# Splitting two layer norms between VectorE and GpSimd, with two tiny reads and another order of value rows, in a dual-stream attention block

## The chip, the cores and the metric

The kernel runs on one core of a Trainium2 chip. A core has a matrix engine (TensorE, in the profile PE, with its weight loads as PEld), VectorE (DVE), ScalarE (ACT), GpSimd (POOL) and SyncE (SP), and sixteen DMA engines that move data between HBM and the core's SBUF. The metric is the device time of one execution in microseconds (us); lower is better.

## The reference

Two streams, an image (2 x 256 tokens) and a text (2 x 32 tokens), 1152 features, all in bfloat16. Both are normalised and modulated, projected to q, k, v, attended together, projected out, gated and added to the input:

```
mod = silu(c) @ wmod                     # shift, scale, gate (image and text have their own)
h   = layernorm(x) * (1 + scale) + shift
q, k, v = split(h @ wqkv)                # image and text tokens joined
a   = softmax(q k^T / sqrt(1152)) v
out = x + gate * (a @ wo)
```

## The kernel before, in words

The instructions of each engine run in the order in which the program writes them; the tile framework adds the semaphores. The 512 image tokens are four tiles of 128 tokens (i = 0 to 3, two to a batch element, `TPB` = 2), the 1152 features nine blocks of 128 (`KT` = 9, kt = 0 to 8). All weights stream once from HBM, nearly all through SP's queue, in the order of the `dma_start` calls. An early transfer's semaphore is one of eight that are used in turn, so that a transfer waits until the one eight places ahead has landed.

The part that the change touches is the first 31 us, in which the image's values `v_i` are computed:

- Loads (lines 80 to 116): `c`, then x tiles 0 and 1 on ScalarE's queue; on SP's queue the image scale weights `w_sc_i` in four column chunks (`KC`: feature blocks 0-1, 2-3, 4-5, 6-8) and between them x tile 2, the value weights `w_v_i` by feature block and x tile 3. Blocks 6, and 7 with 8, are loaded at the end (line 110).
- Layer norm of one tile: `stats_of` (three `bn_stats`, line 169), `std_of` (aggregate on VectorE, Sqrt on ScalarE, line 176), `out_of` (line 182: reciprocal and one VectorE `tensor_scalar` from `x_i` to `xn_i`; columns can be given).
- Transposes on TensorE bring feature blocks to partitions. `x_heads(i)` transposes blocks 0 and 1 (`H` = 2) and `head_scaled` evacuates them on ScalarE with the scale applied; `x_tails(i)` transposes blocks 2 to 8 and `tail_out` copies them out of PSUM unscaled, in two pieces, for tile 0 on ScalarE and for tile 1 on VectorE. Their scale is applied later in SBUF by `apply_mod` (line 262 VectorE, 267 GpSimd, 271 ScalarE), once `mod_scale(ch)` has computed it (54 small matmuls of line 223; for the last chunk `mod_scale_last`, line 245).
- Value matmuls: `v_row(i, kt)` adds feature block kt of tile i into two PSUM banks (512 columns each, line 282); `v_narrow` does the last 128 columns of all tiles in a bank of their own (line 294). `v_wide(i, half, k0, k1)` does one bank over several blocks. PSUM tiles come from a pool of seven banks (`ps_mm`) and one further bank (`ps_sm`).
- `last_transposes` brings tile 3, whose scale is applied as VectorE evacuates it (line 309).

The order before: statistics of tiles 0 and 1, their norms, heads and tails of tile 0, heads and tails of tile 1, tail copies while tile 2 is normalised, then value rows 0 and 1 for tiles 0 and 1, heads of tile 2, second scale chunk, values of tile 2, its tails, and so on through the chunks. At the end row 6 for three tiles, then for each tile rows 7 and 8 together; the transposes of tile 3 stand behind tile 1.

Behind this stage TensorE goes on with the shift strip, the image's q and k (line 529), text rows, scores (619), attention (759) and the output (851). The weights of those stages are loaded by `load_w`, in one to three pieces (`K2` is two pieces, blocks 0-4 and 5-8; `K3` three). A tile that a piece belongs to is used when the pieces it needs have landed. `xf_full` is a tile for the text residual, 2 x 288 columns with 64 unused columns behind them.

Of the kernel before, what the change touches and what calls it, by code (L numbers as in the profile page):

```python
# [9 lines left out]
ALU = mybir.AluOpType  # L10
# [4 lines left out]
def kernel(  # L15
# [14 lines left out]
    nc = tc.nc  # L30
# [4 lines left out]
    B, NI, D = x_img.shape  # L35
    NT = x_txt.shape[1]
    P = 128
    KT = D // P
    NTOK = NI + NT
    NIT = (B * NI) // P  # L40
    TPB = NI // P
    NTT = B * NT
    CH = 384
    NCH = D // CH
# [25 lines left out]
    def w_view(src):  # L70
        return src.rearrange("(kt p) n -> p kt n", p=P)

    def load_w(src, c0, ksplits=((0, KT),), home=None):
        t = wpool.tile([P, KT, D], bf, tag="w", name="t") if home is None else act.tile([P, KT, D], bf, tag=home, name="w_home")
        for (k0, k1) in ksplits:
            nc.sync.dma_start(t[:, k0:k1, :], w_view(src)[:, k0:k1, c0:c0 + D])
        return t
# [11 lines left out]
    def load_x(i, eng=nc.sync):  # L89
        eng.dma_start(x_i[:, i, :], xi_t[:, i, :])  # L90

    def load_sc(ch):
        k0, k1 = KC[ch]
        nc.sync.dma_start(w_sc_i[:, :, k0 * P:k1 * P], w_view(wmod_img)[:, :, D + k0 * P:D + k1 * P])
# [4 lines left out]

    for i in range(TPB):  # L100
        load_x(i, nc.scalar)
    load_sc(0)
    load_x(2)
    load_v(0)
    for ch in range(1, len(KC)):
        load_sc(ch)
        if ch < len(KC) - 1:
            load_v(ch)
    for k0, k1 in ((6, 7), (7, KT)):
        nc.sync.dma_start(w_v_i[:, k0:k1, :], w_view(wqkv_img)[:, k0:k1, 2 * D:3 * D])  # L110
        if k1 < KT:
            load_x(3)
    K3 = ((0, 3), (3, 6), (6, KT))
    K2 = ((0, 5), (5, KT))
# [83 lines left out]
    def x_heads(i):  # L198
        pool, tag = (ps_sm, "sm") if i == 1 else (ps_mm, "mm")
        tp = pool.tile([P, H, P], bf, tag=tag, name="tph")  # L200
        for kt in range(H):
            nc.tensor.transpose(tp[:, kt, :], xn_i[:, i, kt * P:(kt + 1) * P], ident[:])
        return tp

    def head_scaled(tp, i):
        for kt in range(H):
            nc.scalar.activation(hT_i[:, kt, i * P:(i + 1) * P], tp[:, kt, :], ACT.Identity,
                                 scale=mod_i[:, kt, i // TPB:i // TPB + 1])

    def x_tails(i):  # L210
        pool, tag = (ps_mm, "mm") if i < TPB else (ps_sm, "sm")
        tp = pool.tile([P, KT - H, P], bf, tag=tag, name="tp")
        for kt in range(H, KT):
            nc.tensor.transpose(tp[:, kt - H, :], xn_i[:, i, kt * P:(kt + 1) * P], ident[:])
        return tp

    def tail_out(i, tp, k0, k1, on_vector=False):
        (nc.vector.tensor_copy if on_vector else nc.scalar.copy)(hT_i[:, k0:k1, i * P:(i + 1) * P], tp[:, k0 - H:k1 - H, :])
# [71 lines left out]
    def v_narrow(i, k0, k1):  # L290
        if i == 0 and k0 == 0:
            vacc["n"] = ps_mm.tile([P, NIT, P], f32, tag="mm", name="van")
        for kt in range(k0, k1):
            nc.tensor.matmul(vacc["n"][:, i, :], lhsT=hT_i[:, kt, i * P:(i + 1) * P], rhs=w_v_i[:, kt, NM:D],  # L294
                             start=(i == 0 and kt == 0), stop=(i == NIT - 1 and kt == KT - 1))

    def v_row(i, kt):
        v_wide(i, 0, kt, kt + 1)
        v_wide(i, 1, kt, kt + 1)
# [17 lines left out]
    def stats_of(i, k0, k1):  # L317
        lns[i] = ln_stats(x_i[:, i, :], P, k0, k1, lns.get(i))

    def std_of(i):  # L320
        lns[i] = ln_std(lns[i], P)

    def out_of(i, c0=0, c1=D):
        ln_apply(x_i[:, i, :], P, xn_i[:, i, :], *lns[i], c0, c1)

    stats_of(0, 0, NCH)
    std_of(0)
    stats_of(1, 0, NCH)
    std_of(1)
    out_of(0)  # L330
    mod_scale(0, "act")
    out_of(1)
    tails = []
    for i in range(TPB):
        heads = x_heads(i)
        tails.append(x_tails(i))
        head_scaled(heads, i)
    stats_of(2, 0, NCH)
    tail_out(0, tails[0], H, H + 3)
    std_of(2)  # L340
    tail_out(0, tails[0], H + 3, KT)
    tail_out(1, tails[1], H, H + 3, on_vector=True)
    out_of(2, 0, H * P)
    tail_out(1, tails[1], H + 3, KT, on_vector=True)
    out_of(2, H * P, D)
    for kt in range(*KC[0]):
        for i in range(TPB):
            v_row(i, kt)
    for i in range(TPB):
        v_narrow(i, *KC[0])  # L350
    head2 = x_heads(2)
    mod_scale(1, "dve")
    head_scaled(head2, 2)
    apply_mod(2, 0, 2, False, 0)
# [32 lines left out]
    stats_of(3, 0, NCH)  # L387
    std_of(3)
    out_of(3)
    k0 = KC[3][0]  # L390
    for i in range(3):
        v_row(i, k0)
        v_narrow(i, k0, k0 + 1)
    for i in range(3):
        for half in range(2):
            v_wide(i, half, k0 + 1, KT)
        v_narrow(i, k0 + 1, KT)
        if i == 1:
            last_transposes(0, KT - 1, ps_sm, "sm")
            last_transposes(KT - 1, KT, ps_mm, "mm")  # L400
    v_wide(3, 0, 0, KT)
    v_narrow(3, 0, KT)
# [54 lines left out]

    w_k_i = load_w(wqkv_img, D, K3)
    w_sh_t = load_w(wmod_txt, 0)
    w_sc_t = load_w(wmod_txt, D, K2)  # L460
    nc.sync.dma_start(x_t[0:P:P // NTT, :], xt_flat[:, :])
    w_q_t = load_w(wqkv_txt, 0, K2)
    w_k_t = load_w(wqkv_txt, D, K2)
    w_ga_i = load_w(wmod_img, 2 * D, K2, home="V")
    w_v_t = load_w(wqkv_txt, 2 * D, K3)
    w_o_i = load_w(wo_img, 0, K2)
    w_ga_t = load_w(wmod_txt, 2 * D)
# [461 lines left out]
```

## Time and profile before

| | |
|---|---|
| median of 3 runs | 114.62 us (114.5 to 114.75) |
| the profiled execution's own time | 114.88 us |
| its span, first to last instruction | 113.1 us |
| TensorE busy | 108.3 us (96%) |
| VectorE busy | 76.1 us (67%) |
| ScalarE busy | 36.6 us (32%) |
| GpSimd busy | 28.4 us (25%) |
| DMA | 40.87 MB, mean 361 GB/s |

The timeline gives for each group of instructions its start and length in us, the engine, the source line, the operation, output and inputs, the count, and in square brackets how long the engine stood idle before it and what ended that. "q" behind an engine's name is its sequencer, which issues transfers. A matmul's recorded length contains its latency, so neighbouring matmuls overlap in the record. The chain of waits runs backwards from the last instruction; each line of it is start, length, what.

### The profile page before, as it was taken

How to read it: one execution, taken by the hardware profiler on the slowest of the kernel's cores; microseconds unless marked ns; L12 is line 12 of the kernel's file. 1: busy time of each engine (PE TensorE's matmuls, PEld its weight loads, DVE VectorE, ACT ScalarE, POOL GpSimd, SP SyncE). 2: the span in 40 equal slices, each digit the busy share in tenths (PEclk: the TensorE clock that was granted, in tenths of full speed). 3: DMA queues.
4: the chain of work that ended last, by engine and by line, in shares of the span. 5: the costliest groups of instructions: out<-in, count | busy, mean ns of one | idle time of the engine just before them, and what ended most of it. 6: DMA issues, size and time to landing. Idle time of an engine off the chain costs nothing.

```text
span 113.1 us, 2863 instructions
## 1 busy us (share of the span) xinstructions
PE 108.3 (96%) x1195; PEld 64.0 (57%) x1204; DVE 76.1 (67%) x151; ACT 36.6 (32%) x83; POOL 28.4 (25%) x65
## 2 busy tenths in 40 slices
PE   5999999999999999999999999999999999999990
PEld 1356655555444444444446558787687556567670
DVE  1699330956399999999999950237666802995971
ACT  4537500372190071740008924025646700001000
POOL 7100120730140000000000060601550470699300
PEclk9999999999999999999999999999999999999998
DMA  3999999999999999999999999999999999994052
GB/s 92 343 333 355 375 375 405 412 411 408 407 412 412 410 411 402 413 410 412 412 411 415 408 405 407 408 392 394 407 411 397 412 408 406 371 375 161 0 191 70
DMA packets 22839, 40.87 MB, mean 361 GB/s; under 512 B 1375, under 2 KB 6635, under 8 KB 22827
## 3 DMA queue, kind: packets, MB, share of 16 engines
q1 hardware_dynamic: 21547, 39.05, 90.4%
q10 hardware_dynamic: 672, 0.77, 2.2%
q0 software_dynamic: 608, 0.88, 2.1%
q8 instruction: 9, 0.15, 0.5%
q14 instruction: 3, 0.02, 0.1%
HBM read 39.36 MB, written 1.34 MB: 360 GB/s over the span
## 4 chain that ended last, share of the span: by engine, by line
PE 80%; DMA 13%; SPq 4%; issue 1%; DVE 0%
PE qkps L529 31%; PE ps L851 16%; DMA w_sc_i<-in_wmod_img_dram 13%; PE va L282 7%; PE aps L759 5%; PE ps L590 4%; PE sps L619 4%; PE gps L429 3%; SPq L98 3%; PE ops L869 2%; PE ps L694 2%; PE van L294 1%; PE gps L824 1%; PE sps L632 1%; PE pk L703 1%
## 5 line engine op out<-in xcount | busy, mean ns | idle before, releaser
L529 PE MATMUL qkps<-hT_i,t 128*128 128x512 bf16 x158 | 35.4, 379 | 0.2
L529 PEld LDWEIGHTS <-t 128*128 128x128 bf16 x162 | 15.6, 98 | 18.7 <-issue 0.4
L491 DVE SCALAR_TENSOR_TENSOR sacc<-w_v_i,mcols,sacc 128x1152 f32<-128x1152 bf16 x16 | 22.7, 1418 | 0.5
L282 PE MATMUL va<-w_v_i,hT_i 128*128 128x512 bf16 x67 | 17.0, 379 | 0.5 <-issue 0.3
L851 PE MATMUL ps<-t,aT 128*128 128x384 bf16 x99 | 16.4, 326 | 0.0
L851 PEld LDWEIGHTS <-aT 128*128 128x128 bf16 x117 | 11.0, 98 | 6.8 <-issue 0.5
L282 PEld LDWEIGHTS <-hT_i 128*128 128x128 bf16 x72 | 6.4, 98 | 6.2 <-issue 0.2
L835 POOL TENSOR_TENSOR w_og<-t,gb 128x384 bf16<-128x384 bf16 x9 | 8.7, 999 | 4.5 <-DMA gb<-mod_scratch 4.5
L857 DVE TENSOR_TENSOR tmp<-ps,gb 128x384 bf16<-128x384 f32 x11 | 6.0, 550 | 5.6 <-DMA gb<-mod_scratch 5.0
L548 POOL TENSOR_SCALAR mod_txt<-mcols 128x18 f32<-128x18 f32 x2 | 0.6, 275 | 32.4 <-DVE mcols L435 32.4
L169 DVE BATCH_NORM_STATS2 stats<-x_i 128x6 f32<-128x384 bf16 x12 | 5.8, 541 | 2.6 <-DMA x_i<-in_x_img_dram 2.6
L143 PE MATMUL wps<-wz 128*128 128x512 bf16 x15 | 6.1, 578 | 1.2 <-DVE wz L125 1.2
L479 ACT ACTIVATE qT<-qkps 128x512 bf16<-128x512 f32 x9 | 4.7, 600 | 6.9 <-PE qkps L529 6.9
L495 ACT CAST shi<-sacc 128x1152 bf16<-128x1152 f32 x2 | 2.3, 1154 | 13.2 <-DVE sacc L491 13.2
L772 DVE TENSOR_SCALAR aT<-aps,sv 128x288 bf16<-128x288 f32 (+2 forms) x11 | 4.3, 455 | 2.0 <-PE aps L759 2.0
L590 PEld LDWEIGHTS <-t 128*128 128x128 bf16 x162 | 5.0, 98 | 0.5
L157 DVE CAST kT<-qkps 128x512 bf16<-128x512 f32 x3 | 2.1, 686 | 4.7 <-PE qkps L529 4.7
L590 PE MATMUL ps<-hT_t,t 128*128 128x64 bf16 x162 | 5.0, 193 | 0.0
L858 DVE TENSOR_TENSOR o<-tmp,x_i 128x384 bf16<-128x384 bf16 x11 | 4.7, 426 | 0.4
L759 PE MATMUL aps<-pT,v_i 128*128 128x288 bf16 (+2 forms) x44 | 4.8, 264 | 0.0
L774 ACT ACTIVATE aT<-aps,sv 128x288 bf16<-128x288 f32 (+2 forms) x11 | 4.0, 468 | 2.1 <-PE aps L759 2.1
L619 PE MATMUL sps<-kT,qT 128*128 128x288 bf16 x36 | 4.6, 286 | 0.0
(160 smaller groups left out, 139.7 us busy)
## 6 DMA issues: line engine op xcount, KB each, us to landing
t<-in_wqkv_img_dram SPq DMA_DIRECT2D x6, 864.0 KB, 13.2
t<-in_wmod_txt_dram SPq DMA_DIRECT2D x2, 2592.0 KB, 17.6
t<-in_wqkv_txt_dram SPq DMA_DIRECT2D x2, 1440.0 KB, 14.2
t<-in_wmod_img_dram SPq DMA_DIRECT2D x3, 864.0 KB, 12.3
t<-in_wqkv_txt_dram SPq DMA_DIRECT2D x3, 864.0 KB, 14.1
t<-in_wo_txt_dram SPq DMA_DIRECT2D x3, 864.0 KB, 15.5
t<-in_wqkv_txt_dram SPq DMA_DIRECT2D x2, 1152.0 KB, 15.0
w_v_i<-in_wqkv_img_dram SPq DMA_DIRECT2D x7, 288.0 KB, 6.9
```

Source lines behind the costliest of these rows:

```text
L143: nc.tensor.matmul(ps[:], lhsT=wz[:, 0:P], rhs=wz[:], start=True, stop=True)
L169: nc.vector.bn_stats(stats[0:np_, k, :], x_ap[:, k * CH:(k + 1) * CH])
L282: nc.tensor.matmul(ps[:], lhsT=hT_i[:, kt, i * P:(i + 1) * P], rhs=w_v_i[:, kt, half * VW:(half + 1) * VW], start=(kt == 0), stop=(kt == K ...
L479: nc.scalar.mul(out_ap, in_ap, SCALE)
L491: nc.vector.scalar_tensor_tensor(saccs[b][:], w_v_i[:, kt, :], ap, saccs[b][:], op0=ALU.mult, op1=ALU.add)
L529: nc.tensor.matmul(pss[j - j0][:], lhsT=wq[:, kt, j * P:(j + 1) * P], rhs=hT_i[:, kt, :], start=(kt == 0), stop=(kt == KT - 1))
L590: nc.tensor.matmul(ps[:, j - j0, :], lhsT=wq[:, kt, j * P:(j + 1) * P], rhs=hT_t[:, kt, :], start=(kt == 0), stop=(kt == KT - 1))
L619: nc.tensor.matmul(sps[:], lhsT=qkTs[0][:, ft, b, q0:q0 + P], rhs=qkTs[1][:, ft, b, :], start=(ft == 0), stop=(ft == KT - 1))
L759: nc.tensor.matmul(bank[:, off:off + c1 - c0], lhsT=lhsT, rhs=rhs, start=(first[id(bank)] == n), stop=(final[id(bank)] == n))
L835: nc.gpsimd.tensor_mul(w_og[:, dt, 0:CH], w_o_i[:, dt, NG0:D], gb[:, B - 1, NG0:D])
L851: nc.tensor.matmul(ps[:, 0:cw], lhsT=aT[:, dt, t0:t0 + P], rhs=rhs, start=(dt == DTS[0]), stop=(dt == DTS[-1]))
L857: nc.vector.tensor_mul(tmp[:, 0:cw], ps[:, 0:cw], gb[:, b, cs])
```

## The change

- Two more transfers on ScalarE's queue behind x tiles 0 and 1. Each reads 2 elements from 16 rows into unused columns of `xf_full`: every sixteenth row of x tiles 2 and 3, and every eighth of the first 128 rows of the value weights. Nothing reads what they bring.
- Value weights' feature blocks 7 and 8 are loaded one by one.
- Tiles 1 and 2: VectorE normalises columns 0 to 255 and GpSimd columns 254 to 1151. Both write columns 254 and 255, so GpSimd's instruction follows VectorE's.
- The heads of tiles 0 and 1 come first and are scaled in turn (block 0 of both, then block 1 of both). Tile 0's tails stand behind the first value row, tile 1's behind the fourth; tile 0's tail copies on ScalarE stand behind the Sqrt for tile 2.
- At the end of the value rows, row 7 of tiles 0 and 1 is done on its own ahead of row 8. The eight first transposes of tile 3 stand behind tile 0 instead of tile 1.
- Three text and gate weights (`w_sc_t`, `w_q_t`, `w_ga_i`) are loaded in one piece instead of two.

```diff
@@ -99,6 +99,8 @@
     for i in range(TPB):
         load_x(i, nc.scalar)
+    nc.scalar.dma_start(xf_full[0:16, 2 * VC + 2:2 * VC + 4], xi_flat[2 * P:4 * P:16, 0:2])
+    nc.scalar.dma_start(xf_full[0:16, 2 * VC:2 * VC + 2], wqkv_img[0:P:8, 2 * D:2 * D + 2])
     load_sc(0)
@@ -106,9 +108,9 @@
-    for k0, k1 in ((6, 7), (7, KT)):
-        nc.sync.dma_start(w_v_i[:, k0:k1, :], w_view(wqkv_img)[:, k0:k1, 2 * D:3 * D])
-        if k1 < KT:
+    for kt in range(*KC[-1]):
+        nc.sync.dma_start(w_v_i[:, kt:kt + 1, :], w_view(wqkv_img)[:, kt:kt + 1, 2 * D:3 * D])
+        if kt == KC[-1][0]:
             load_x(3)
@@ -202,8 +204,8 @@
-    def head_scaled(tp, i):
-        for kt in range(H):
+    def head_scaled(tp, i, k0=0, k1=H):
+        for kt in range(k0, k1):
@@ -323,32 +325,39 @@
+    def head_and_rest(i):
+        mv, rstd = lns[i]
+        out_of(i, 0, H * P)
+        nc.gpsimd.tensor_scalar(xn_i[:, i, H * P - 2:D], x_i[:, i, H * P - 2:D], mv[:, 0:1], rstd[:],
+                                op0=ALU.subtract, op1=ALU.mult)
+
     mod_scale(0, "act")
-    out_of(1)
-    tails = []
+    head_and_rest(1)
+    heads = [x_heads(i) for i in range(TPB)]
+    for kt in range(H):
+        for i in range(TPB):
+            head_scaled(heads[i], i, kt, kt + 1)
+    stats_of(2, 0, NCH)
+    v_row(0, 0)
+    tails = [x_tails(0)]
+    std_of(2)
+    tail_out(0, tails[0], H, H + 3)
+    tail_out(0, tails[0], H + 3, KT)
+    head_and_rest(2)
+    v_row(1, 0)
     for i in range(TPB):
-        heads = x_heads(i)
-        tails.append(x_tails(i))
-        head_scaled(heads, i)
-    stats_of(2, 0, NCH)
-    tail_out(0, tails[0], H, H + 3)
-    std_of(2)
-    tail_out(0, tails[0], H + 3, KT)
+        v_row(i, 1)
+    tails.append(x_tails(1))
     tail_out(1, tails[1], H, H + 3, on_vector=True)
-    out_of(2, 0, H * P)
     tail_out(1, tails[1], H + 3, KT, on_vector=True)
-    out_of(2, H * P, D)
-    for kt in range(*KC[0]):
-        for i in range(TPB):
-            v_row(i, kt)
+    head2 = x_heads(2)
     for i in range(TPB):
         v_narrow(i, *KC[0])
-    head2 = x_heads(2)
     mod_scale(1, "dve")
@@ -387,16 +396,20 @@
-    k0 = KC[3][0]
     for i in range(3):
-        v_row(i, k0)
-        v_narrow(i, k0, k0 + 1)
+        v_row(i, KT - 3)
+        v_narrow(i, KT - 3, KT - 2)
+    for i in range(TPB):
+        v_row(i, KT - 2)
+        v_narrow(i, KT - 2, KT - 1)
     for i in range(3):
+        k0 = KT - 1 if i < TPB else KT - 2
         for half in range(2):
-            v_wide(i, half, k0 + 1, KT)
-        v_narrow(i, k0 + 1, KT)
+            v_wide(i, half, k0, KT)
+        v_narrow(i, k0, KT)
+        if i == 0:
+            last_transposes(0, KT - 1, ps_sm, "sm")
         if i == 1:
-            last_transposes(0, KT - 1, ps_sm, "sm")
             last_transposes(KT - 1, KT, ps_mm, "mm")
@@ -457,11 +470,11 @@
-    w_sc_t = load_w(wmod_txt, D, K2)
+    w_sc_t = load_w(wmod_txt, D)
-    w_q_t = load_w(wqkv_txt, 0, K2)
+    w_q_t = load_w(wqkv_txt, 0)
-    w_ga_i = load_w(wmod_img, 2 * D, K2, home="V")
+    w_ga_i = load_w(wmod_img, 2 * D, home="V")
```

## The prediction

> **What bounds the kernel now.** I read the page first, then the chain of waits, then the timeline of the first 32 us.
>
> ```profile
> span 113.1 us, 2863 instructions
> ```
>
> ```profile
> 10.29 8.84 DMA w_sc_i<-in_wmod_img_dram
> ...
> 19.18 0.57 PE sps L245 x36
> ...
> 67.69 2.36 PE ps L590 x81
> ...
> 79.02 0.01 PE gps L636 x2
> ```
>
> The profiled run took 114.88 us, 1.78 us of them outside the span; the median of the runs is 114.62. I work out a difference on the profiled execution and add it to the median. In the chain of waits there is one large thing that is not TensorE: the last column chunk of w_sc_i, issued at 10.29 and landed 8.84 later at 19.13. TensorE's matmuls of line 245 start on it, and from there TensorE follows itself almost to the end. So an edit pays only if it lets line 245 start earlier, or shortens TensorE's own row of work behind it.
>
> ```profile
> 18.89 0.23 PE L240 MATMUL sps<-ones_full 128*32 128x96 bf16 x4
> ```
>
> This is the work in front of line 245 (timeline of TensorE). TensorE is there at 18.89 and starts at 19.18: **0.29 us of slack**. That is all that can be saved there without an earlier landing, and the first 0.29 us by which the early work becomes later cost nothing.
>
> **The early stage.** Rows of the timeline, in the order of time:
>
> ```profile
> 7.90 0.58 DVE L182 TENSOR_SCALAR xn_i<-x_i,mv,rstd 128x1152 bf16<-128x1152 bf16 x1
> ...
> 8.24 1.25 ACT L207 ACTIVATE hT_i<-tph,mod_img 128x128 bf16<-128x128 bf16 x4 [0.22 <-PE tph L202]
> 8.39 1.47 DVE L169 BATCH_NORM_STATS2 stats<-x_i 128x6 f32<-128x384 bf16 x3
> 8.53 0.11 PEld L202 LDWEIGHTS <-xn_i 128*128 128x128 bf16 x2 [0.18 <-DVE xn_i L182]
> ...
> 9.05 1.89 PE L282 MATMUL va<-w_v_i,hT_i 128*128 128x512 bf16 x7
> ...
> 9.37 0.48 ACT L218 COPY hT_i<-tp 128x384 bf16<-128x384 bf16 x1
> ...
> 10.05 0.29 DVE L218 COPY hT_i<-tp 128x384 bf16<-128x384 bf16 x1
> ...
> 10.17 0.29 ACT L176 ACTIVATE rstd<-mv,eps_t 128x1 f32<-128x1 f32 x1 [0.32 <-DVE mv L174]
> ...
> 10.37 0.57 ACT L218 COPY hT_i<-tp 128x512 bf16<-128x512 bf16 x1
> ...
> 10.70 0.34 DVE L182 TENSOR_SCALAR xn_i<-x_i,mv,rstd 128x256 bf16<-128x256 bf16 x1
> ...
> 10.96 0.42 DVE L218 COPY hT_i<-tp 128x512 bf16<-128x512 bf16 x1
> ...
> 11.23 0.59 PE L223 MATMUL mps<-sT,w_sc_i 128*128 128x2 bf16 x18
> 11.30 0.50 DVE L182 TENSOR_SCALAR xn_i<-x_i,mv,rstd 128x896 bf16<-128x896 bf16 x1
> 11.43 0.63 ACT L207 ACTIVATE hT_i<-tph,mod_img 128x128 bf16<-128x128 bf16 x2 [0.49 <-PE tph L202]
> 11.85 0.65 PE L282 MATMUL va<-w_v_i,hT_i 128*128 128x512 bf16 x2
> ...
> 12.45 0.55 PE L214 MATMUL tp<-ident,xn_i 128*128 128x128 bf16 x7
> ```
>
> A record's length holds its latency, so I use pitches. Line 282 at 9.05: eight matmuls in the code, seven recorded, the last 0.38 long: (1.89 - 0.38)/7 = 0.216 a matmul. Transposes: (0.55 - 0.22)/6 = 0.055, which I also take for the narrow matmuls (as wide). Line 223: (0.59 - 0.16)/17 = 0.025.
>
> Both orders meet again at tile 2's tail transposes, now at 12.45. From the first value matmul to there TensorE now does 8 + 2 wide matmuls (2.16), 6 narrow ones and 2 transposes (0.44), and 18 of line 223 (0.45): 3.05 us. 9.05 + 3.05 = 12.10, so 0.35 us of it is waiting.
>
> After the change the fourteen tail transposes of tiles 0 and 1 (14 x 0.055 = 0.77) stand among the value rows and not ahead of them: 3.82 us. The first value row waits for ScalarE's first scaled head: 8.24 + 1.25/4 = 8.55, and 0.10 of signal, as at 11.85, where line 282 follows the first of the two activations of 11.43 (11.43 + 0.63/2 = 11.75). Start 8.65, meeting point 8.65 + 3.82 = 12.47. **The reordering by itself is worth nothing (+0.02):** the value rows start 0.40 earlier and carry 0.77 more work; the 0.35 of waits is what it eats.
>
> Then the new waits. VectorE's part of tile 1 ends at 7.90 + 0.34 = 8.24 and not 8.48, so everything on VectorE behind it is 0.24 early: the Sqrt for tile 2 at 9.93. But ScalarE now has that Sqrt ahead of tile 0's tail copies, one of which stands at 9.37 today: 9.93 + 0.29 + 0.48 + 0.57 = 11.27 instead of 10.94. Tile 1's tails are transposed last (about 11.16), so VectorE's copies of them end near 11.45 + 0.29 + 0.42 = 12.16, and not at 10.96 + 0.42 = 11.38. The tiles `van` and `va20` need PSUM banks, and both sets of tails hold one. TensorE wants the banks at 11.27 and 12.03. If the banks freed first are taken first, it waits 0.1 and then up to 0.15 more; if `head2`'s or another is free, nothing. I take 0.2 of the 0 to 0.25: the meeting point is 12.67, 0.22 late.
>
> **GpSimd's 898 columns.** No row shows them. These do (groups by form, GpSimd):
>
> ```profile
> L835 POOL TENSOR_TENSOR w_og<-t,gb 128x384 bf16<-128x384 bf16 x9 | 8.7, 999 | 4.5 <-DMA gb<-mod_scratch 4.5
> ...
> L267 POOL TENSOR_SCALAR hT_i<-hT_i,mod_img 128x128 bf16<-128x128 bf16 x2 | 0.7, 379 | 3.3 <-DVE mod_img L231 3.3
> ...
> L267 POOL TENSOR_SCALAR hT_i<-hT_i,mod_img 128x256 bf16<-128x256 bf16 x1 | 0.5, 484 | 8.5 <-ACT hT_i L207 8.5
> ```
>
> The same operation costs (484 - 379)/128 = 0.82 ns a column: 484 + 642 x 0.82 = 1.01 us. The upper bound is the two-input rate, 999/384 = 2.6 ns: 2.3 us. The lower bound is VectorE's 0.50 for 896 columns. I take 1.01, the same operation. Tile 1: 8.35 to 9.4, wanted near 10.8: hidden. Tile 2: VectorE's head ends 0.24 earlier than 10.70 + 0.34, at 10.80; GpSimd 10.9 to 11.9, wanted at 12.47 to 12.67: hidden with 0.6 to spare. Behind it on GpSimd stands the scaling of row 3, free again before row 3's scales exist.
>
> TensorE thus reaches line 240 0.22 later, at 19.11, inside the 0.29.
>
> **The transfers.** ScalarE issues two more (0.87 us for two, below) ahead of its table loads; the first thing that can notice is the Sqrt at 5.58, which waits 0.83 for VectorE:
>
> ```profile
> 0.74 0.87 ACTq L90 DMA_DIRECT2D x_i<-in_x_img_dram  x2
> ...
> 5.58 0.29 ACT L176 ACTIVATE rstd<-mv,eps_t 128x1 f32<-128x1 f32 x1 [0.83 <-DVE mv L174]
> ```
>
> So the issuing costs 0 to 0.04. What the sixteen 4-byte reads each may bring is an earlier touch of x tiles 2 and 3 and of w_v's first row tile. Windows (the last figures are the DMA's busy share and GB/s):
>
> ```profile
> 6.30:7.60 1.30, 1.30 (x21) 0.70 (x19) 1.23 (x5) 0.29 (x1) 0.00 (x0) 1.00 1.07 353
> ...
> 18.00:19.00 1.00, 1.00 (x13) 0.62 (x12) 0.00 (x0) 0.00 (x0) 0.00 (x0) 1.00 1.05 409
> ```
>
> At the same busy share the first big packets move 353 and later ones 409 GB/s. Tile 2 and the first two value rows are 0.885 MB: 2.51 against 2.16 us. Cured wholly, 0.35 us earlier for all that follows; nothing, if the slowness is not a first touch; a loss of 0.1 (a packet in the way) below. Only a part of those bytes is touched ahead: I take 0.1. Line 245 then starts at the later of 19.08 and 19.12: **-0.06**.
>
> **The last value rows.** The same wait for normalised tile 3 gates both orders (timeline; the last two rows are the load of rows 7 and 8 and its line's times to landing):
>
> ```profile
> 21.87 0.22 PE L294 MATMUL van<-w_v_i,hT_i 128*128 128x128 bf16 x1
> 22.05 1.02 PE L282 MATMUL va<-w_v_i,hT_i 128*128 128x512 bf16 x4
> ...
> 23.00 0.58 DVE L182 TENSOR_SCALAR xn_i<-x_i,mv,rstd 128x1152 bf16<-128x1152 bf16 x1
> ```
>
> ```profile
> 13.58 0.43 SPq L110 DMA_DIRECT2D w_v_i<-in_wqkv_img_dram  x1
> ```
>
> ```profile
> DMA to landing us min/median/max: 8.4/8.7/9.0
> ```
>
> Rows 7 and 8 landed at 13.58 + 8.4 = 22.0, and line 282 started at 22.05 where 21.87 + 0.055 = 21.93 was possible: a wait of 0.12. Split, row 7 lands 295 KB earlier, 0.7 us: the wait goes. But the eight transposes of tile 3 move from behind two tiles to behind one. TensorE gets to them at 21.93 + 3 x (2 x 0.216 + 0.055) = 23.39; the tile is ready at 23.58, and 0.05 later for TensorE (8.48 to 8.53 above): a new wait of 0.24. Both chains hang on line 245 alike. **Net +0.12.** It falls to 0 if tile 3 is ready earlier.
>
> **The merged loads** cost nothing if their last half, which lands as before, is in time (page and SP's timeline):
>
> ```profile
> t<-in_wqkv_txt_dram SPq DMA_DIRECT2D x2, 1152.0 KB, 15.0
> ...
> w_home<-in_wmod_img_dram SPq DMA_DIRECT2D x1, 1152.0 KB, 14.0
> ```
>
> ```profile
> 45.51 3.21 SPq L76 DMA_DIRECT2D t<-in_wqkv_txt_dram  x2
> ```
>
> ```profile
> 59.58 2.48 SPq L76 DMA_DIRECT2D w_home<-in_wmod_img_dram  x2
> ```
>
> w_q_t: at the latest 45.51 + 3.21 + 15.0 = 63.7 against its use at 67.69. w_ga_i: 59.58 + 2.48 + 14.0 = 76.1 against 79.02. w_sc_t is ahead of w_q_t in the queue. Two transfers more, one more and three fewer leave the count, and so the turn of the later transfers' semaphores, as it was.
>
> **Sum:** -0.06 + 0.12 = +0.06. 114.62 + 0.06 = **114.7 us**: no change. A measurement of this kernel tells 0.2%, 0.23 us, from none. Bounds of this case: 114.4 to 115.0.
>
> **Rivals.** (1) *GpSimd becomes the bound* (slower). At the two-input rate the second rest ends at 10.9 + 2.3 = 13.2, the tail transposes of tile 2 start 13.3 and not 12.67, and line 240 is reached at 18.89 + 0.85 = 19.74, 0.56 past 19.18. With the 0.12: +0.68, 115.3. It decides from 12.67 on, a rest of 1.7 us or 1.9 ns a column. For it: 898 columns are far from 256. Against it: the slope of line 267. The same happens if VectorE and GpSimd hold each other up, and for that there are rows:
>
> ```profile
> L262 DVE TENSOR_SCALAR hT_i<-hT_i,scols 128x128 bf16<-128x128 bf16 x1 | 0.5, 481 | 0.0
> ...
> L262 DVE TENSOR_SCALAR hT_i<-hT_i,mod_img 128x128 bf16<-128x128 bf16 x2 | 0.4, 250 | 1.6 <-ACT hT_i L218 1.6
> ```
>
> The same VectorE instruction took 481 beside GpSimd's line 267 and 250 without. The Trainium skill (SBUF — State Buffer, "Who interferes with whom") says that the pair of ports is an exclusive lock, so that the later one blocks fully; by that rule VectorE's scaling of row 2 would stand behind the whole rest. It costs only if the rest runs past 12.3, as here. Chance, with smaller waits of that place (banks at their worst): 0.32.
>
> (2) *The touch works* (faster). Landing 0.35 earlier, no bank waits (meeting point 12.47, line 240 at 18.91, or 0.1 less if signals are shorter than mine), tile 3 ready as TensorE comes: line 245 at 18.85, -0.33, 114.3. For it: 353 against 409 GB/s. Against: it needs three terms at their good ends. 0.23.
>
> (3) *It does not do what it says*: the overlap of columns 254 and 255 orders GpSimd behind VectorE only, and the tiny reads touch nothing useful. Then the landing stays 19.13: +0.12, inside the forecast's 0.45.
>
> **Numbers.** The forecast's 0.45 splits 0.07 faster, 0.31 same, 0.07 slower; with the rivals 0.30, 0.31, 0.39. Its own range 114.4 to 115.0; the range for 8 in 10 reaches to both rivals, 114.15 to 115.4.
>
> **What would show it.** Right: first line 282 near 8.65; tile 2's tails near 12.5 to 12.7; GpSimd's rests near 1.0 us; line 245 within 0.1 of 19.1; a short idle of TensorE before line 306 at about 23.4, none before row 7. Wrong: rests over 1.7 us; the chunk landing before 18.9 or after 19.3; TensorE waiting for a merged load; the transposes of tile 3 without a wait.

## The result, and the profile after

| | before | after |
|---|---|---|
| median (6 runs each) | 114.66 us (114.5 to 114.79) | 127.53 us (126.48 to 128.29) |
| profiled execution | 114.88 us, span 113.1 | 128.29 us, span 126.5 |
| mean granted clock of TensorE | 0.997 | 0.96 |

The ratio is 1.1119, 95% interval 1.1069 to 1.117: the change costs 12.9 us where the prediction had +0.06. Line numbers of the changed kernel are 2 to 13 higher than before (line 245 is 247, 282 is 284, 529 is 542). Three profiles below, of runs e3, e5 and e10, are of executions 1.5, 1.5 and 2.1 us longer than their kernels' medians; lengths, waits and transfer rates are read from them, no total times.

The loss has two parts, which the same two kinds of rows show. The first is GpSimd and TensorE in the timeline of the changed kernel, first 18 us:

```profile
8.36 3.40 POOL L331 TENSOR_SCALAR xn_i<-x_i,mv,rstd 128x898 bf16<-128x898 bf16 x1 [4.03 <-DVE xn_i L184]
13.84 3.38 POOL L331 TENSOR_SCALAR xn_i<-x_i,mv,rstd 128x898 bf16<-128x898 bf16 x1 [2.07 <-DVE xn_i L184]
```

```profile
11.82 0.23 PE L204 MATMUL tph<-ident,xn_i 128*128 128x128 bf16 x1 [3.29 <-POOL xn_i L331]
11.88 0.59 PE L284 MATMUL va<-w_v_i,hT_i 128*128 128x512 bf16 x2
...
12.92 2.76 PE L284 MATMUL va<-w_v_i,hT_i 128*128 128x512 bf16 x6
...
17.27 0.23 PE L204 MATMUL tph<-ident,xn_i 128*128 128x128 bf16 x1 [0.99 <-POOL xn_i L331]
...
25.26 0.56 PE L247 MATMUL sps<-w_sc_i,sT 128*32 128x96 bf16 x36
```

GpSimd's 898 columns take **3.40 us, not 1.01**. And what waits for them is not the tails of tile 2 but the *heads*: the second transpose of line 204 takes block 1, columns 128 to 255, and columns 254 and 255 are those that GpSimd writes too. TensorE stands 3.29 us in front of tile 1's head. Behind that pause its clock falls: the first two value matmuls still stand 0.59 - 0.38 = 0.21 us apart, the six that follow (2.76 - 0.6)/5 = 0.43 instead of 0.216, and the clock row of the page has one slice of 3.16 us, from 12.65 us on, at half:

```profile
PEclk9999599999999999999999999999999999965899
```

The chain of waits shows that tile 2 cannot start meanwhile: ScalarE's Sqrt for tile 2 stands behind the scaled heads of tile 1, which stand behind that transpose (start, length, what):

```profile
8.36 3.41 POOL xn_i L331
...
11.82 0.24 PE tph L204
...
12.09 0.88 ACT hT_i L209 x3
12.97 0.19 ACT rstd L178
...
13.84 3.39 POOL xn_i L331
```

Line 247 starts at 25.26 to 25.43 instead of 19.18, and the attention's end, marked by the loads of `gb`, is 95.36 - 89.18 = 6.18 us late. The second part stands behind that point. GpSimd's timeline, first of before, then of after:

```profile
89.18 1.14 POOL L809 DMA_DIRECT2D gb<-mod_scratch  x2 [4.68 <-PE aps L759]
90.31 2.17 POOL L812 DMA_DIRECT2D xf_full<-in_x_txt_dram  x4
96.99 8.70 POOL L835 TENSOR_TENSOR w_og<-t,gb 128x384 bf16<-128x384 bf16 x9 [4.52 <-DMA gb<-mod_scratch]
```

```profile
95.36 1.14 POOL L822 DMA_DIRECT2D gb<-mod_scratch  x2 [4.66 <-PE aps L772]
101.38 2.17 POOL L825 DMA_DIRECT2D xf_full<-in_x_txt_dram  x4 [4.88 <-issue]
103.57 7.85 POOL L848 TENSOR_TENSOR w_og<-t,gb 128x384 bf16<-128x384 bf16 x9
```

A gap of 4.88 us, with nothing that GpSimd waits for, stands between the loads of `gb` and those of `xf_full`; before there is none. By the time that GpSimd comes to its nine products, `gb` is there, so it does not stop in front of them. VectorE, whose additions get in behind one product after another before, is now shut out (timeline of VectorE before, then of VectorE and of TensorE after):

```profile
97.78 0.48 DVE L858 TENSOR_TENSOR o<-tmp,x_i 128x384 bf16<-128x384 bf16 x1
```

```profile
102.27 0.36 DVE L871 TENSOR_TENSOR o<-tmp,x_i 128x384 bf16<-128x384 bf16 x1
...
103.13 8.51 DVE L871 TENSOR_TENSOR o<-tmp,x_i 128x384 bf16<-128x384 bf16 x1
```

```profile
112.16 0.43 PE L882 MATMUL ops<-t,aT 128*32 128x288 bf16 x4 [3.80 <-DVE tmp L870]
113.02 4.27 PE L882 MATMUL ops<-t,aT 128*32 128x288 bf16 x68 [0.43 <-DVE tmp L870]
```

One addition of 0.36 us takes 8.51. PSUM is not emptied, TensorE waits 3.80, and after the pause its clock is down again (slices at .6, .5, .8): the 68 matmuls of line 882 that are left take 4.27 us, where the chain of before has 2.21 for all 72:

```profile
102.15 2.21 PE ops L869 x72
```

They start 113.02 - 102.15 = 10.87 later than before, 4.69 more than the 6.18; 4.27 - 2.21 = 2.06 and, in the last products, 6.49 - 5.99 = 0.50 come on top. 6.18 + 4.69 + 2.06 + 0.50 = 13.43, and the two profiled executions differ by 128.29 - 114.88 = 13.41.

### The profile page after: what moved, and what is told of

Same layout as the page of the kernel before. It is cut to its first block, busy times and chain, and to the rows that moved or that the text cites. A ratio compares the mean times of both kernels' runs of the same rounds, so it can differ in the third digit from the quotient of the medians.

```text
span 126.5 us, 2875 instructions
## 1 busy us (share of the span) xinstructions
PE 113.2 (89%) x1204; PEld 65.8 (52%) x1204; DVE 82.4 (65%) x150; ACT 36.7 (29%) x83; POOL 34.4 (27%) x67
## 4 chain that ended last, share of the span: by engine, by line
PE 62%; DVE 12%; DMA 8%; issue 7%; POOL 5%; ACT 2%; ACTq 0%; POOLq 0%; DVEq 0%
PE qkps L542 28%; PE va L284 9%; DVE o L871 7%; POOL xn_i L331 5%; PE ps L864 5%; DMA gb<-mod_scratch 5%; PE ps L603 4%; PE sps L632 4%; PE ops L882 3%; PE gps L442 3%; DMA x_i<-in_x_img_dram 3%; DVE tmp L870 2%; PE ps L707 2%; ACT hT_i L209 1%; DVE stats L171 1%
## 5 line engine op out<-in xcount | busy, mean ns | idle before, releaser
L284 PE MATMUL va<-w_v_i,hT_i 128*128 128x512 bf16 x72 | 19.0, 400 | 0.1
L864 PE MATMUL ps<-t,aT 128*128 128x384 bf16 x99 | 16.9, 333 | 0.0
L871 DVE TENSOR_TENSOR o<-tmp,x_i 128x384 bf16<-128x384 bf16 x11 | 12.1, 1099 | 0.4
L882 PE MATMUL ops<-t,aT 128*32 128x288 bf16 x72 | 4.7, 444 | 4.2 <-DVE tmp L870 4.2
L331 POOL TENSOR_SCALAR xn_i<-x_i,mv,rstd 128x898 bf16<-128x898 bf16 x2 | 6.8, 3393 | 6.1 <-DVE xn_i L184 6.1
L848 POOL TENSOR_TENSOR w_og<-t,gb 128x384 bf16<-128x384 bf16 x9 | 7.8, 907 | 0.0
L145 PE MATMUL wps<-wz 128*128 128x512 bf16 x15 | 5.6, 540 | 1.2 <-DVE wz L127 1.2
L882 PEld LDWEIGHTS <-aT 128*32 128x32 bf16 x72 | 3.1, 143 | 5.6 <-issue 4.8
L204 PE MATMUL tph<-ident,xn_i 128*128 128x128 bf16 x6 | 1.2, 226 | 5.0 <-POOL xn_i L331 4.3
```

Source lines behind the costliest of these rows:

```text
L145: nc.tensor.matmul(ps[:], lhsT=wz[:, 0:P], rhs=wz[:], start=True, stop=True)
L284: nc.tensor.matmul(ps[:], lhsT=hT_i[:, kt, i * P:(i + 1) * P], rhs=w_v_i[:, kt, half * VW:(half + 1) * VW], start=(kt == 0), stop=(kt == K ...
L331: nc.gpsimd.tensor_scalar(xn_i[:, i, H * P - 2:D], x_i[:, i, H * P - 2:D], mv[:, 0:1], rstd[:], op0=ALU.subtract, op1=ALU.mult)
L848: nc.gpsimd.tensor_mul(w_og[:, dt, 0:CH], w_o_i[:, dt, NG0:D], gb[:, B - 1, NG0:D])
L864: nc.tensor.matmul(ps[:, 0:cw], lhsT=aT[:, dt, t0:t0 + P], rhs=rhs, start=(dt == DTS[0]), stop=(dt == DTS[-1]))
L871: nc.vector.tensor_add(o[:, cs], tmp[:, 0:cw], x_i[:, i, cs])
```

## The experiments

**e1: the whole change, but VectorE does the rest of the norm.** Does all the loss hang on GpSimd?

```diff
-        nc.gpsimd.tensor_scalar(xn_i[:, i, H * P - 2:D], x_i[:, i, H * P - 2:D], mv[:, 0:1], rstd[:],
-                                op0=ALU.subtract, op1=ALU.mult)
+        out_of(i, H * P, D)
```

> The changed kernel with VectorE doing columns 256 on of tiles 1 and 2, GpSimd doing none of the norm; the tiny reads, the new order, the single last rows and the merged loads stay. Theory (everything that was lost hangs on the two GpSimd instructions: 6.2 us early, because TensorE's second head transpose reads columns 128 to 255 and so waits for the instruction that also writes 254 and 255, and about 7 us late, because GpSimd's program got longer): line 245 near 19.1 us, GpSimd's loads of the text residual issued straight behind those of the gate, total 114.3 to 115.0. Rival (the tiny reads into the text residual's tile hold back GpSimd's later loads of that tile): early loss gone, late loss stays, about 121.

115.08 us, ratio 1.0033 (1.0013 to 1.0052), 0.08 over the expected. Both parts are gone: line 247 starts at 19.36, and `xf_full` follows `gb` at once (timelines of TensorE and GpSimd):

```profile
19.36 0.56 PE L247 MATMUL sps<-w_sc_i,sT 128*32 128x96 bf16 x36
```

```profile
90.65 2.16 POOL L824 DMA_DIRECT2D xf_full<-in_x_txt_dram  x4
```

Two GpSimd instructions make 12.4 of the 12.9 us; all else in the change is worth +0.3%.

**e2: GpSimd from column 256 on, so that no column is shared.**

```diff
-        nc.gpsimd.tensor_scalar(xn_i[:, i, H * P - 2:D], x_i[:, i, H * P - 2:D], ...
+        nc.gpsimd.tensor_scalar(xn_i[:, i, H * P:D], x_i[:, i, H * P:D], ...
```

> The changed kernel with GpSimd's columns starting at 256 and not 254, so that nothing it writes is read by the head transposes. Theory (the overlap is what stops TensorE): the two waits of 3.3 and about 1 us of the head transposes on GpSimd go, GpSimd's instruction still takes about 3.4 us, the tails then wait 0.5 to 1.5 us each; line 245 near 20.5 to 21.5 instead of 25.4; the late loss stays; total 122.5 to 124.5. Rival (GpSimd's 3.4 us come from the odd start column or from the overlap itself): the instruction falls to about 1 us and line 245 comes to 19.1; total 121.

123.58 us, ratio 1.0754 (1.0692 to 1.0816). GpSimd's timeline:

```profile
8.65 6.78 POOL L331 TENSOR_SCALAR xn_i<-x_i,mv,rstd 128x896 bf16<-128x896 bf16 x2 [4.13 <-DVE rstd L183]
...
98.18 2.16 POOL L825 DMA_DIRECT2D xf_full<-in_x_txt_dram  x4 [4.88 <-issue]
```

The shared columns cost 4.0 us at this length of GpSimd's instruction (127.53 - 123.58). Still 3.39 us for each, so the odd start column is not what makes them slow, and the late gap is untouched. Line 247 came at 22.00, later than expected: one instruction behind the other, the second ends at 15.43 and tile 2's tails hang on it.

**e3: the kernel before with four more GpSimd instructions.** The gap of 4.88 us has no wait behind it, but where it stands an instruction packet is in the records. The DMA view counts packets by kind in a window (queue, kind, packets, MB, share); before between 95 and 97 us, after between 99 and 101.4:

```profile
q14 instruction: 1, 0.01, 1.0%
```

```profile
q14 instruction: 1, 0.01, 0.8%
```

My theory became: GpSimd fetches its next block of instructions at a fixed place of its program; the change puts two norms and two waits ahead, so that the place moves from behind the four `xf_full` loads, where the wait for `gb` covers the fetch, to in front of them.

```diff
+    pad4 = const.tile([P, 4], bf)
+    for n in range(4):
+        nc.gpsimd.memset(pad4[:, n:n + 1], 0.0)
```

> The kernel before with four one-column memsets more on GpSimd at the start (0.1 us each, in idle time), nothing else. Theory (the late loss is where in GpSimd's program its next block of instructions has to be fetched: four instructions more move that point from behind the loads of the text residual to in front of them): the same gap of nearly 5 us on GpSimd between the gate's and the residual's loads, then VectorE held up by GpSimd's weight products; 118 to 122. Rival (the late loss comes of the early one, another meeting of transfers and engines): 114.6, as before.

125.45 us, ratio 1.0907 (1.0864 to 1.095): the gap is there, but the loss is far over what was expected.

```profile
94.54 1.13 POOL L812 DMA_DIRECT2D gb<-mod_scratch  x2 [5.12 <-PE aps L762]
100.88 2.16 POOL L815 DMA_DIRECT2D xf_full<-in_x_txt_dram  x4 [5.21 <-issue]
```

The loads of `gb` are already 5.4 us late, so something else was changed too. The windows show it, 30 to 60 us, of before and of e3 (the last figure is the DMA's GB/s):

```profile
30.00:60.00 30.00, 29.73 (x144) 13.52 (x140) 29.22 (x31) 9.16 (x18) 1.62 (x3) 1.00 1.04 410
```

```profile
30.00:60.00 30.00, 30.00 (x170) 13.84 (x163) 28.22 (x30) 8.75 (x17) 1.61 (x3) 1.00 1.05 391
```

At the same busy share the DMA moves 391 instead of 410 GB/s. The edit does one thing more than was meant: the new tile of 8 bytes a partition moves every tile behind it. So e3 tests two things and settles neither.

**e4 and e5: fewer instructions, and four more without a new tile.** e4 is the changed kernel with five of GpSimd's start memsets on VectorE, e5 the kernel before with four one-column memsets into a tile that is there already.

```diff
# e4
-    nc.gpsimd.memset(ones32, 0.0)      # and four more
+    nc.vector.memset(ones32, 0.0)
# e5
+    for n in range(4):
+        nc.gpsimd.memset(x_t[:, n:n + 1], 0.0)
```

> The changed kernel with five of GpSimd's memsets at the start done by VectorE, so that GpSimd's program is again about as long as before in front of the late loads. Theory (place of the fetch): the early loss of 6.2 us stays, line 245 near 25.4; the late gap of nearly 5 us goes; total 120 to 121.5. Rival (late loss follows from the early one or from the tiny reads): 127.5, no change.

> The kernel before with four one-column memsets more on GpSimd, this time into columns of the text tile that is cleared there anyway, so that no tile of SBUF moves (the earlier run's new tile of 8 bytes moved all tiles behind it, and its large DMA packets took 96 to 107 ns where 93 are usual). Theory (place of GpSimd's next fetch): gap of nearly 5 us before the residual's loads at about 95 us, VectorE held up behind GpSimd's weight products, packets at 93 ns; 120 to 122. Rival (the moved tiles did all of it): 114.7.

e4: 121.09 us, ratio 1.0542 (1.0512 to 1.0572). e5: 120.83 us, ratio 1.0498 (1.0457 to 1.054). Both as expected. GpSimd's timeline of e4, then of e5:

```profile
95.72 1.14 POOL L822 DMA_DIRECT2D gb<-mod_scratch  x2 [4.98 <-PE aps L772]
96.85 2.16 POOL L825 DMA_DIRECT2D xf_full<-in_x_txt_dram  x4
103.50 8.77 POOL L848 TENSOR_TENSOR w_og<-t,gb 128x384 bf16<-128x384 bf16 x9 [4.49 <-DMA gb<-mod_scratch]
```

```profile
89.38 1.14 POOL L811 DMA_DIRECT2D gb<-mod_scratch  x2 [4.80 <-PE aps L761]
95.36 2.17 POOL L814 DMA_DIRECT2D xf_full<-in_x_txt_dram  x4 [4.85 <-issue]
97.55 7.85 POOL L837 TENSOR_TENSOR w_og<-t,gb 128x384 bf16<-128x384 bf16 x9
```

The early loss stays whole in e4 (line 247 at 25.29) and the late one goes; in e5 the early stage is that of before and **four memsets without any work in them cost 6.1 us**, 80 us later, by the number of GpSimd's instructions alone. In the records of after, e2, e3, e5 and e13 the instruction packet starts 3.0 to 3.2 us behind the start of the gap.

**e7: e5 with the `xf_full` loads issued at 72 us**, ahead of the gap and away from it.

```diff
+        for g in range(NGG):                  # behind the loads of v_t
+            nc.gpsimd.dma_start(xf[32 * g:32 * g + 32, :, :], xt_q[g])
...
-    for g in range(NGG):                      # behind the loads of gb
-        nc.gpsimd.dma_start(xf[32 * g:32 * g + 32, :, :], xt_q[g])
```

> The run before this (four memsets, no tile moved) with the four loads of the text residual issued by GpSimd behind the loads of v_t at about 72 us instead of behind the gate's. Theory (the fetch costs only because transfers stand behind it and the weight products then start late): the fetch now falls where GpSimd waits for the gate anyway; 114.5 to 115.2. Rival (any fetch in that stretch costs its 5 us, or the longer program itself is slow): 119 or more.

115.42 us, ratio 1.0057 (1.0038 to 1.0076), 0.2 over the expected. Moving the loads has moved the place of the fetch too: the packet now stands at 87.0 us, ahead of the loads of `gb`, where GpSimd waits 4.51 us for TensorE anyway (4.68 before). So the fetch is covered again, though by another wait than was expected, and the products wait for `gb` as they do before:

```profile
96.77 8.68 POOL L837 TENSOR_TENSOR w_og<-t,gb 128x384 bf16<-128x384 bf16 x9 [6.15 <-DMA gb<-mod_scratch]
```

The Trainium skill (Runtime: NRT & Kernel Launch, "Instruction fetch mechanics") has an engine's program streamed in blocks of 256 instructions and calls the crossing "mostly hidden". That the packet's place moves with the number of instructions agrees; the size of a block no run here shows. That it is hidden does not agree: it is 4.85 to 4.88 us here (5.21 in e3), in the open as soon as no wait covers it.

**e6 and e13: why 3.4 us?** Instructions alone, in the kernel before, into an unused part of `x_t`; the times of these kernels are not read. e6 asked for two pointers, or the length of the row; e13 for the subtraction, its place, or the operand.

> The kernel before with five GpSimd tensor_scalar instructions more behind line 422, on x tile 0, results into the text tile that is cleared and used later: 896 columns with one pointer operand (multiply, add 0), 896 with one pointer (subtract, times 1), 256 and 128 with two pointers, 256 with one. Theory (two pointer operands make the slow form): 896 with one pointer near 1.0 us (0.82 ns a column), 256 with two near 1.0 us and 128 near 0.55 (3.7 ns a column). Rival (long rows are slow, whatever the operands): 896 with one pointer near 3.4 us, 256 with two near 0.5. The total time says nothing here.

> The kernel before with four GpSimd instructions of 896 columns in a row, each into the unused part of x_t: (x + mean) rstd; (x - rstd) 1.0; x rstd - mean; x rstd rstd. So far subtract then multiply took 3.3 to 3.4 us and multiply then add 1.0 to 1.1. Theory 1 (the subtraction is what is slow, wherever it stands): 1.0 to 1.2, 3.2 to 3.5, 3.2 to 3.5, 1.0 to 1.2. Theory 2 (only multiply then add has a fast path): 3.2 to 3.5 for the first three, the fourth open. Theory 3 (the operand mean was what was slow, not the operation): 3.2 to 3.5 for the first and the third, 1.0 to 1.2 for the second and the fourth; the 1.10 of e9, which adds a value in the same tile, speaks against it. The run's total time is not read.

Groups of e6 by form, then GpSimd's timeline of e13; 424 to 428 are, in e6, x rstd + 0, (x - mean) 1.0, twice (x - mean) rstd, x rstd + 0, and in e13 424 to 427 (x + mean) rstd, (x - rstd) 1.0, x rstd - mean, x rstd rstd:

```profile
L424 POOL TENSOR_SCALAR x_t<-x_i,rstd 128x896 bf16<-128x896 bf16 x1 | 1.0, 1011 | 0.0
```

```profile
28.03 3.29 POOL L425 TENSOR_SCALAR x_t<-x_i,mv 128x896 bf16<-128x896 bf16 x1
31.43 1.22 POOL L426 TENSOR_SCALAR x_t<-x_i,mv,rstd 128x256 bf16<-128x256 bf16 x1
32.75 0.79 POOL L427 TENSOR_SCALAR x_t<-x_i,mv,rstd 128x128 bf16<-128x128 bf16 x1
33.64 0.48 POOL L428 TENSOR_SCALAR x_t<-x_i,rstd 128x256 bf16<-128x256 bf16 x1
```

```profile
23.52 1.08 POOL L424 TENSOR_SCALAR x_t<-x_i,mv,rstd 128x896 bf16<-128x896 bf16 x1
24.69 3.29 POOL L425 TENSOR_SCALAR x_t<-x_i,rstd 128x896 bf16<-128x896 bf16 x1
28.09 3.36 POOL L426 TENSOR_SCALAR x_t<-x_i,rstd,mv 128x896 bf16<-128x896 bf16 x1
31.55 1.12 POOL L427 TENSOR_SCALAR x_t<-x_i,rstd 128x896 bf16<-128x896 bf16 x1
```

Both theories of e6 missed: one pointer is as slow as two, and short rows are slow in proportion ((1.22 - 0.79)/128 = 3.4 ns a column). e13 is a clean answer: **the subtraction is slow, wherever it stands and whichever operand it takes** (3.29, 3.36); additions and multiplications, with one pointer or two, take 1.01 to 1.12 for 896 columns, near the 0.82 ns a column and 0.28 us that line 267 had shown. The starts of neighbours (24.69 to 28.09 to 31.55) confirm the lengths.

**e8: the last value rows and their loads alone.**

```diff
-    for k0, k1 in ((6, 7), (7, KT)):
+    for kt in range(*KC[-1]):           # one load for each block; row 7 of tiles 0 and 1 ahead of row 8,
...                                      # the transposes of tile 3 behind tile 1 as before
-    w_sc_t = load_w(wmod_txt, D, K2)
+    w_sc_t = load_w(wmod_txt, D)
```

> The kernel before with the value weights' blocks 7 and 8 loaded one by one and row 7 of tiles 0 and 1 ahead of row 8, but the transposes of tile 3 left behind tile 1 (and one text weight in one piece, so that the number of transfers stays). Theory (the wait of 0.12 us before row 7 goes and no wait for tile 3 takes its place): 0.05 to 0.2 us faster than before. Rival (the order of these rows is of no account): within 0.05 us.

114.73 us, ratio 0.9992 (0.9972 to 1.0011): no difference that can be told, and the interval holds both expectations. Its profile has no wait in front of row 7, but there line 245 starts at 19.78 instead of 19.18, which gives the loads 0.6 us more; e11 below, with the loads of before, has none there either. So it is not shown that the split loads removed it.

**e9 and e10: the change with its causes of loss mended.** The norm as x rstd + (-mean rstd), columns from 256 on, five start memsets on VectorE; e10 is e9 from column 254 on.

```diff
+        nc.vector.tensor_scalar(mv[:, 1:2], mv[:, 0:1], rstd[:], -1.0, op0=ALU.mult, op1=ALU.mult)
-        nc.gpsimd.tensor_scalar(xn_i[:, i, H * P - 2:D], x_i[:, i, H * P - 2:D], mv[:, 0:1], rstd[:],
-                                op0=ALU.subtract, op1=ALU.mult)
+        nc.gpsimd.tensor_scalar(xn_i[:, i, H * P:D], x_i[:, i, H * P:D], rstd[:], mv[:, 1:2],
+                                op0=ALU.mult, op1=ALU.add)
```

> The changed kernel with its three causes of loss mended and the work still on GpSimd: the norm written as x times rstd plus (-mean rstd), which a one-number VectorE instruction prepares; columns from 256 on, so none is shared with the heads; five start memsets on VectorE, so that the program of GpSimd is no longer than before. My theory (the placement of the forecast held, and form, shared columns and program length were what failed): GpSimd's two instructions of 896 columns take 0.9 to 1.1 us each, line 247 starts between 19.1 and 19.5, the transfers xf_full stand straight behind gb, and the time is 114.7 to 115.3, as with VectorE's rest (115.08). Rival (two pointers per instruction are slow in any form): 2.2 to 3.4 us each, line 247 at 21 or later, 116.5 to 119. Second rival (GpSimd and VectorE hold each other up in this stage whatever the form): GpSimd near 1.0, but VectorE's instructions beside it over twice as long, line 247 at 19.6 to 20.5, 115.4 to 116.3.

> As the run before, but from column 254 on, as in the change: the price of the two shared columns alone. My theory (the second head's transpose waits for GpSimd's whole instruction): TensorE's transposes of tiles 1 and 2 (line 204) each wait for POOL by about 1 us, line 247 starts 0.8 to 1.5 later than in the run before, and the time is 0.8 to 1.6 above it (115.6 to 116.7). Rival (with an instruction of 1 us the wait hides behind the value rows and the slack in front of line 247): line 247 within 0.3 and the time within 0.4 of the run before.

e9: 115.17 us, ratio 1.0034 (1.0022 to 1.0046), as expected. Its timelines, GpSimd and TensorE:

```profile
8.41 1.10 POOL L332 TENSOR_SCALAR xn_i<-x_i,rstd,mv 128x896 bf16<-128x896 bf16 x1 [4.00 <-DVE mv L331]
11.09 1.10 POOL L332 TENSOR_SCALAR xn_i<-x_i,rstd,mv 128x896 bf16<-128x896 bf16 x1 [1.58 <-DVE mv L331]
```

```profile
8.59 0.61 PE L284 MATMUL va<-w_v_i,hT_i 128*128 128x512 bf16 x2
...
12.64 0.55 PE L216 MATMUL tp<-ident,xn_i 128*128 128x128 bf16 x7
...
19.15 0.56 PE L247 MATMUL sps<-w_sc_i,sT 128*32 128x96 bf16 x36
...
23.30 0.22 PE L296 MATMUL van<-w_v_i,hT_i 128*128 128x128 bf16 x1
23.60 0.62 PE L308 MATMUL tp<-ident,xn_i 128*128 128x128 bf16 x8
```

e10: 116.88 us, ratio 1.0194 (1.0164 to 1.0225). The two shared columns alone cost 1.71 us, a little over the expected 0.8 to 1.6. TensorE's wait for them is in its timeline, at tile 1 alone; the one expected at tile 2 is not there. Where line 247 starts is not read from this profile:

```profile
10.68 0.23 PE L204 MATMUL tph<-ident,xn_i 128*128 128x128 bf16 x1 [1.12 <-POOL xn_i L332]
```

**e11, e12, e14, e15, e16: where the last 0.3% is.** e11 is the kernel before with the two tiny transfers. e12 is e1 with the last value rows and their loads as before. e14 is e9 with the three merged loads split again. e15 is e11 with two loads merged, so that the number of transfers is that of before. e16 is the kernel before with all that the change does to transfers, and its order of work untouched.

```diff
# e11
+    nc.scalar.dma_start(xf_full[0:16, 2 * VC + 2:2 * VC + 4], xi_flat[2 * P:4 * P:16, 0:2])
+    nc.scalar.dma_start(xf_full[0:16, 2 * VC:2 * VC + 2], wqkv_img[0:P:8, 2 * D:2 * D + 2])
# e15: e11 and
-    w_sc_t = load_w(wmod_txt, D, K2)
-    w_q_t = load_w(wqkv_txt, 0, K2)
+    w_sc_t = load_w(wmod_txt, D)
+    w_q_t = load_w(wqkv_txt, 0)
# e16: e15, w_ga_i in one piece, and one load for each of value blocks 7 and 8
```

> The kernel before with the two tiny transfers alone. My theory (they touch nothing that was slow; the last chunk of w_sc_i lands where it did): line 245 within 0.15 of 19.2 and 114.6 to 114.9. Rival (first touch, as the prediction's rival 2 had it): line 245 at 18.9 or earlier, 114.4 or less. Second rival (they get in the way, and are the 0.3% that the rest of the change cost): line 245 at 19.4 or later, 115.0 or more.

> The changed kernel with VectorE's rest (115.08), and the last value rows and their loads as before the change. If the last rows (the transposes of tile 3 now in front of tile 3's normalising) cost the 0.3%, as my prediction's +0.12 had it: 114.7 to 114.9, with no wait of TensorE in front of line 308. If it is the early order or the merged loads: 115.0 to 115.3.

> The kernel of e9 with the three merged loads split in two again. If the merged loads are what leaves e9 0.34% above the kernel before: ratio 0.999 to 1.002. If they cost nothing, as my prediction had it: ratio 1.0025 to 1.0045, as in e9.

> The kernel before with the two tiny transfers, and two loads merged (w_sc_t, w_q_t), so that the number of transfers is that of before. In e11 (tiny transfers alone, two transfers more) the last chunk of w_sc_i was there 0.28 us earlier and TensorE ended 0.41 earlier, but SyncE's waits at the end of the program met the last stores in another order, and the span was no shorter. Theory A (the early landing comes from the tiny transfers, and only the end gave it back): line 245 near 18.9, span 112.6 to 112.8, 114.3 to 114.55, ratio 0.996 to 0.9985. Theory B (18.90 was that execution's chance): line 245 near 19.2, ratio 0.999 to 1.002.

> The kernel before with all that the change does to transfers (two tiny ones, the last value rows loaded singly, three loads merged; the number as before) and none of what it does to the order of the work or to GpSimd. If the 0.34% that e9 keeps comes from the order of the work (tile 3's transposes a tile earlier, my +0.12): ratio 0.996 to 1.001. If it comes from the transfers: 1.002 to 1.005.

| run | median us | ratio | 95% | line 245 or 247 at | span |
|---|---|---|---|---|---|
| e11 | 114.93 | 1.0011 | 0.9996 to 1.0026 | 18.90 | 113.1 |
| e12 | 114.90 | 1.0023 | 1.0005 to 1.004 | 19.61 | 113.4 |
| e14 | 116.07 | 1.0114 | 1.0093 to 1.0134 | 19.07 | 114.0 |
| e15 | 114.81 | 0.9993 | 0.9978 to 1.0007 | 19.24 | 113.2 |
| e16 | 114.57 | 0.9983 | 0.9968 to 0.9997 | 19.01 | 112.9 |

e15 went by theory B: with the tiny transfers the chunk was there at 19.24 in one execution and by 18.90 in another (e11). In e5 and e8, which have no tiny transfers, that line starts at 18.94 and 19.78, so 18.90 is that execution's chance, and the time is that of before. e16 has all the change's transfers and is no slower, if anything 0.2 us faster. So the 0.34% of e9 does not come from the transfers; e1 has it (0.33%) without GpSimd's instructions, and what both share beside the transfers is the order of the work. e12 says little: its interval holds both expectations.

Both expectations of e14 missed: splitting three loads costs 0.9 us against e9. TensorE's work is not later (VectorE's last addition starts at 110.39 us, 110.38 before); the end is. These are the starts, in the records of SyncE, of its waits for the transfers' semaphores at the end of the program, and the end of the last instruction on any engine:

```
before  111.07 111.14 111.21 111.27 111.34 111.39 111.48 111.92 112.18   end 113.10
e9      111.17 111.24 111.31 111.37 111.43 111.49 111.61 112.02 112.27   end 113.17
e14     111.08 111.50 111.94 112.20 112.26 112.32 112.38 112.44 112.53   end 113.95
e11     110.66 111.50 111.77 111.83 111.90 111.95 112.02 112.08 112.17   end 113.11
```

SyncE waits for the semaphores in a fixed order, 0.06 us each. Where the last store's is late in that order (before, e9), the others are done by then; where it stands early, five waits follow it in e14 and six in e11. They take 0.34 us in e14, and the 0.40 in e11 is where its earlier TensorE (its last addition starts at 109.97) went. Another 0.46 us of e14, between SyncE's two drains behind the waits, is not explained.

## Why the prediction was wrong, point by point

**GpSimd's 898 columns, taken as 1.01 us: the step that failed first.** "The same operation" was not the same: line 267 multiplies and adds, line 331 subtracts and multiplies. Both are called TENSOR_SCALAR in the profile, and the operations are only in the code. It is 3.4 us, over the "upper bound" of 2.3, too, which came from a product of two tiles. In e9, with an addition, it is 1.10. Rival 1 (GpSimd becomes the bound) was the right kind, and its point of decision, a rest of 1.7 us, was passed; its price of 0.68 was far too small, since it let only tile 2's tails wait.

**"Wanted near 10.8: hidden"** for tile 1 failed for another reason: I asked when the *tails* want GpSimd's columns. The heads' second block ends at column 255 and so reads the two columns that both engines write. Rival 3 has the sentence that is wrong: the overlap orders "GpSimd behind VectorE only". It also puts the head's transpose behind GpSimd. That is 4.0 us with the slow form (e2) and 1.7 with the fast one (e10).

**The length of GpSimd's program** is not in the prediction at all. It counted transfers and their semaphores when it said that the count is left, and not the instructions of the engine that was given work. Worth 6.1 us by e5, and 127.53 - 121.09 = 6.4 by e4.

**What held.** With these three mended, e9 is the forecast's kernel. The first value row was forecast at 8.65 and came at 8.59; tile 2's tails 12.47 to 12.67, came 12.64; line 247 "within 0.1 of 19.1", came 19.15; the wait in front of tile 3's transposes 0.24, came 23.60 - (23.30 + 0.055) = 0.245. The 0.2 us lost at the meeting point was given to PSUM banks; in e9's chain no bank is waited for: the value matmuls at 12.10 follow ScalarE's scaled heads of tile 2 (11.42 to 12.06), and these follow TensorE's transposes, which end at 11.40. The merged loads cost nothing, and that the number of transfers is as before mattered more than I knew (e14).

**The sum +0.06 for the rest was too small, though its largest term came.** e1 and e9 are at +0.3% (0.3 to 0.4 us). From line 245 (247) to the first matmul of line 529 (543) TensorE needs 31.29 - 19.18 = 12.11 us before and 31.39 - 19.15 = 12.24 in e9: +0.13, where "Net +0.12" was forecast. Against e16, with the same transfers and the old order, e9's line 247 starts 0.14 later and line 529's matmuls come a further 0.26 later, of which the wait for tile 3 is 0.24. e16 needs 31.00 - 19.01 = 11.99 us for that stretch, without the wait of 0.12 in front of row 7; but e11, with the loads of before, needs 30.89 - 18.90 = 11.99 too. So that wait comes and goes with the execution, the gain of 0.12 by the split loads is not shown, and where the wait is absent e9's net is +0.25. The times of e8 and e15 are too coarse to tell -0.12 and -0.06 from nothing. The -0.06 rests on a misreading besides: line 240's own four matmuls stand in front of line 245 (19.09 to 19.15 in e9), so that the slack was 0.23 and not 0.29, and line 240 reached at 19.11 gives -0.01. About 0.2 us of e9's distance lies outside its span and was not located.

**A version that beats both?** e16 alone lies below the kernel before, by 0.03 to 0.32%, at the limit of what can be told. Moving the norms to GpSimd brings nothing here even when it is done right: e9 (115.17) is no faster than e1 (115.08), in which VectorE does them.

## What to carry to other kernels

Before work is given to another engine, price its exact operation there and not one of the same name, and look in the code for every reader of each column it writes, not only for the reader it is meant for. Count the instructions of the engine that gets the work: its program is fetched in blocks, and four instructions early can put a fetch of 5 us in front of a transfer 80 us later. Where a gap has no releaser, look for an instruction packet in it.

## What the runs showed of the hardware that was not expected

- GpSimd's subtraction costs 3.3 us for 896 columns in bfloat16, an addition or a multiplication 1.1 (e13).
- GpSimd's fetch of instructions is 4.9 us in the open (e5), and nothing in the waits names it.
- One VectorE addition of two SBUF tiles (0.36 us) stood 8.51 us beside nine GpSimd products. In every run the products have waits ahead of the first and of the sixth alone. In the twelve profiles in which GpSimd had stood waiting in front of the first product, the additions got in between them (0.48 us each in e4); in the six in which it came there without a stop (after, e2, e3, e5, e6, e13), one addition stood 7.7 to 8.5 us, until the ninth product had ended. Why the stop decides it is open. The Trainium skill (SBUF — State Buffer, "Who interferes with whom") says that a VectorE instruction with two SBUF inputs contends with a GpSimd instruction that reads SBUF, and that the order of issue decides who blocks. The trace agrees on the block; but in after the addition started at 103.13, ahead of the first product at 103.57, and stood all the same, and over nine instructions, not one.
- With a new tile of 8 bytes a partition the DMA moved 391 GB/s from 30 to 60 us, at the same busy share, and 410 with the same memsets in a tile that was there (e3 against e5). That the moved tiles are the cause is inferred: e5 differs from e3 only in where the memsets write.
- The order in which SyncE waits for the transfers' semaphores at the end is worth 0.3 to 0.4 us (e11, e14), so a change in the number of transfers anywhere can move the time without touching any work.
